# Retention outputs of a block in two visits of TensorE instead of three, and one pair's scores and k^T v' two products earlier

## The chip, the cores and the metric

The kernel runs on one core of a Trainium2 chip. The time is in microseconds on the device, from one execution of the whole program. The profile is of another execution of the same program. In it, TensorE is PE, its weight loads are PEld, VectorE is DVE, ScalarE is ACT, GpSimd is POOL and SyncE, which issues the DMA transfers, is SP. The granted clock of TensorE was 1.000.

## The reference

Two steps follow each other. The first is a retention (linear attention with a decay) over q, k and v of shape 4 x 8 x 768 x 64 (batch, heads, tokens, width of a head):

```python
gamma = 1.0 - 2.0 ** (-5.0 - np.arange(H))
for t in range(S):
    state = gamma * state + einsum('bhd,bhe->bhde', k[:, :, t], v[:, :, t])
    y[:, :, t] = scale * einsum('bhd,bhde->bhe', q[:, :, t], state)
```

Its output becomes x, with 3072 rows (batch and token) and 512 columns (head and width). The second step is two layers with an ELU between them:

```python
h = x @ w_in                                   # 512 -> 2048
g = np.where(h > 0.0, h, np.exp(np.minimum(h, 0.0)) - 1.0)
out = g @ w_out                                # 2048 -> 512
```

All is float32.

## The kernel before, in words

The 3072 tokens are worked on in six blocks of 512 (`TB`). The text calls them the first to the sixth; in the code `tb` is 0 to 5. A block is four chunks of 128 tokens, and two chunks are a pair (`pp` is 0 or 1). The two layers of the first block are plain products. The second block takes one level of Strassen's method in the first layer (`first`) and two in the second (`second_twice`). Blocks three and four, and then five and six, go through together (`big_twice`, `passes`, `second_big`, with `nb` 0 and 1). The large matmuls are 128x128 weights against 128, 256 or 512 columns.

The order of the work is written out by hand. Each engine runs its instructions in the order in which the program emits them. The products are generators: every `yield` is a place where something else can be put between two products.

The retention of a block is put in between like that, while the block or the pair of blocks before it is still in its layers. It works on pieces of 64 tokens, with 64x64 matmuls in two row groups and two column groups of TensorE:

- `scores(tb, pp)`: the products of k and q of a pair (64 small matmuls in the profile for each pair, which it calls `sc`), which VectorE then masks (L342) and writes over k in the chunk's tile.
- `states(tb, pp)`: k^T v' of a pair, where v' is v times a power of the decay (tile `kv`). ScalarE or VectorE add them up to running states (L381, L383).
- `outputs(tb, pp)`: a generator with two stops. To the first it issues `within` (masked scores times v'). To the second it issues `across` for `other` = 0 (q times the state, for two of the four pairings of row group and half). It also lets VectorE copy a few columns of the PSUM tiles `y` into `seen` (L411), for which `across` with `other` = 1 must wait. From there to its end it issues `across` with `other` = 1, and VectorE multiplies `y` by powers of the decay into x (L417).

A pair has two `y` tiles, and `sc`, `kv`, `y` and some results of the layers share the four buffers of the pool `ps_r`. A float32 matmul of the program stands as two matmuls and two weight loads in the profile.

A stretch in which TensorE does only such small matmuls between two products is called a visit here. Before the change the outputs of a block take three visits, by `outputs_step(tb, step)`:

- Blocks two to four (`early_end`): first pair up to its second stop; then the end of the first pair and the second pair up to its second stop; then the end of the second pair.
- Blocks five and six: first pair up to its second stop; second pair up to its second stop; then the ends of both.

`retention_step(tb, n)` calls `scores` for both pairs (n = 0), `states` for both (1), and `outputs_step(tb, n - 2)` for 2 and more. Where these calls stand is said by lists like `VISITS`, whose entries are (number of the product, place in it); places are "first", "middle" and "end". `LOADS` says in the same way where a chunk of the next block is loaded, by a DMA that SP issues (L125), and where GpSimd scales v (L305).

The fourth block's pairs are apart. Before the change `scores(3, 0)` comes when the second block's last product of the second layer has been through its "end" place, and `states(3, 0)`, `scores(3, 1)`, `states(3, 1)` and the outputs come in the first two rounds (`at` = 0 and 1) of the loop over `big_twice`.

Some other names: `bank("a")`, `bank("b")` and `bank("d")` are the PSUM tiles `pa` (two buffers), `pb` and `pd` (one each) of the layers' products. L1376, L1268, L977 and L1330 are matmuls of the layers, L989, L1388 and L1283 are VectorE's additions that read a bank of PSUM, and L944 and L1358 are VectorE's differences that make the inputs of coming products (`ts`, `tq`, `gC`).

Of the kernel before, what the change touches and what calls it, by code (L numbers as in the profile page):

```python
# [28 lines left out]
def kernel(  # L29
# [267 lines left out]
    held = {}  # L297
# [28 lines left out]
    def score_products(sc, tb, pp, x):  # L326
        qk = raw[tb * CPB + 2 * pp + x][0]
        for p in range(HP):
            for sub in range(2):
                for a in range(2):  # L330
                    nc.tensor.matmul(  # L331
                        sc[a][rows(sub), x, p, :], lhsT=qk[rows(a), 1, p, rows(sub)],
                        rhs=qk[rows(a), 0, p, rows(sub)], start=True, stop=True, skip_group_check=True,
                    )

    def scores(tb, pp):

        sc = [ps_r.tile([P, 2, HP, D], FP32, name="sc", tag="r") for _ in range(2)]
        for x in range(2):
            score_products(sc, tb, pp, x)  # L340
        for a in range(2):
            nc.vector.tensor_tensor(  # L342
                out=raw[tb * CPB + 2 * pp + a][0][:, 1].rearrange("p h c -> p (h c)").rearrange("p (n t) -> p n t", t=D),
                in0=sc[a].rearrange("p x h t -> p (x h) t"),
                in1=cmask.unsqueeze(1).to_broadcast([P, 2 * HP, D]), op=ALU.mult,
            )
# [18 lines left out]
    def state_products(kvs, tb, pp, x, subs):  # L365
        kv = raw[tb * CPB + 2 * pp + x][1]
        for p in range(HP):
            for sub in subs:
                for a in range(2):
                    if not fresh(tb, 4 * pp + 2 * x + sub + 1):  # L370
                        nc.tensor.matmul(  # L371
                            kvs[sub][rows(a), x, p, :], lhsT=kv[rows(sub), 1, 2 * p + a, :],
                            rhs=kv[rows(sub), 0, 2 * p + a, :], start=True, stop=True, skip_group_check=True,
                        )

    def state_sum(kvs, tb, pp, x, sub, copy=None):
        n = 4 * pp + 2 * x + sub
        if fresh(tb, n + 1):
            return
        if fresh(tb, n):  # L380
            (copy or nc.scalar.copy)(state(tb, n + 1), kvs[sub][:, x])  # L381
        else:
            nc.vector.tensor_tensor(out=state(tb, n + 1), in0=kvs[sub][:, x], in1=state(tb, n), op=ALU.add)  # L383

    def states(tb, pp):

        kvs = [ps_r.tile([P, 2, HP, D], FP32, name="kv", tag="r") for _ in range(2)]
        for x in range(2):
            state_products(kvs, tb, pp, x, range(2))
        for x in range(2):  # L390
            for sub in range(2):
                state_sum(kvs, tb, pp, x, sub)
# [80 lines left out]
    def outputs_step(tb, step):  # L473

        if step == 0:
            held["y"] = [outputs(tb, pp) for pp in range(2)]
        early_end = tb <= 3
        if step and early_end:
            next(held["y"][step - 1], None)
        elif step == 2:  # L480
            for g in held["y"]:
                next(g, None)
        if step < 2:
            next(held["y"][step])
            next(held["y"][step])

    half = [slice(0, TH), slice(TH, TB)]

# [127 lines left out]
    def small_of_pieces(at):  # L616

        sources = [
            (decoded[2 * NQ + n].rearrange("p r (d c) -> p (r d) c", d=2)[:, 1:4], sums[n])
            for n in (2 * at, 2 * at + 1)  # L620
        ]
        return combine_w_out(at, *sources)
# [915 lines left out]
    y = outputs_of_first()  # L1538
# [40 lines left out]
    y = outputs(0, 1)  # L1579
# [9 lines left out]
    def run(steps):  # L1589
        for _ in steps:  # L1590
            pass

    def next_piece(by_vector=False):
        decode_all()
        prepare(by_vector=by_vector)
# [8 lines left out]
    for n, _ in enumerate(inner):  # L1604
        if n in (0, 2, 4):
            load(CPB + n // 2)
        if n == 4:
            load(CPB + 3)
        if n in (1, 2, 4, 5, 7, 9):
            next_piece(n in (1, 2, 5, 7))  # L1610
        if n == 8:
            scale_v(CPB + 2, True)
        if n in (3, 5, 9):
            scale_v(CPB + (n - 3) // 2)
        if n == 4:
            run(inputs_of_first(0, [hslot() for _ in range(3)]))
        elif n == 10:
            scores(1, 0)
            scores(1, 1)
        elif n == 11:  # L1620
            states(1, 0)
            states(1, 1)
            next_piece()
            parts = sums_of_pieces(0)
            next(parts)
        elif n == 12:
            outputs_step(1, 0)
            run(parts)
            next_piece()
        elif n == 13:  # L1630
            outputs_step(1, 1)
            smalls = small_of_pieces(0)
            some(smalls, 3)
        elif n == 14:
            outputs_step(1, 2)
            some(smalls, 2)
            decode_all()
        elif n == 15:
            run(smalls)
# [40 lines left out]
    def retention_step(tb, step):  # L1680
        if step == 0:
            scores(tb, 0)
            scores(tb, 1)
        elif step == 1:
            states(tb, 0)
            states(tb, 1)
        else:
            outputs_step(tb, step - 2)
# [87 lines left out]
        pass  # L1776
    flush()
    retention_step(2, 2)
    step, VISITS = 0, {(1, "first"): 3, (1, "end"): 4}
    LOADS = {(1, "first"): 0, (2, "end"): 1, (4, "end"): 2, (5, "end"): 3}  # L1780
    for s in sec:
        if s == "first":
            step += 1
        at = (step, s if s in ("first", "middle") else "end")
        if s in ORDER2 and 1 <= step <= 4:
            some(smalls[1], 1 if step < 4 else 3)
        if step == 5:
            send_small(2)
        elif at == (6, "first"):
            sent(1)  # L1790
        if at in VISITS:
            retention_step(2, VISITS[at])
        if at in LOADS:
            load(3 * CPB + LOADS[at])
            scale_v(3 * CPB + LOADS[at])
        if s == ORDER2[-1]:
            break
    scores(3, 0)
    for _ in sec:
        pass  # L1800
    mid.close()
# [5 lines left out]
    for nb in range(NB):  # L1807
        more = nb + 1 < NB
        q6, q4, u3, ends = {}, {}, {}, {}
        groups = 2 * nb + 4, 2 * nb + 5  # L1810
# [79 lines left out]
        for at, (j, sub) in enumerate(ORDER1):  # L1890
            if at == 2:
                held_x = [ldpool.tile([P, 2048], FP32, name="chunk", tag="chunk") for _ in range(2)]
                G["M1"] = [x.rearrange("p (n f t c) -> p n f t c", n=2, f=2, t=2) for x in held_x]
            cur = big_twice(nb, j, sub)
            next(cur)
            if at:
                next(tail, None)
            else:
                run(tail)
                open_lifts()  # L1900
            side(at, 0)
            if at == 1 and nb == 0:
                retention_step(3, 2)
            next(cur)
            side(at, 1)
            if nb == 0:
                if at == 0:
                    states(3, 0)
                elif at == 1:
                    retention_step(3, 3)  # L1910
            run(tail)
            if at == 7:
                seeds(0, 1, first=True)
            next(cur)
            tail = cur
            if nb == 0:
                if at == 0:
                    scores(3, 1)
                    states(3, 1)
                elif at == 1:  # L1920
                    retention_step(3, 4)
                    run(tail)
            side(at, 2)
            if more and at in (5, 6):
                load(groups[0] * CPB + at - 5)
            if nb == 0 and at in stores:
                stores[at]()
                send_small()
# [71 lines left out]
        if more:  # L2000
            for n in range(CPB):
                scale_v(groups[0] * CPB + n)
        step = 0
        VISITS = [
            (0, "end"), (1, "end"), (2, "middle"), (2, "end"), (3, "middle"),
            (5, "first"), (5, "end"), (6, "first"), (6, "middle"), (6, "end"),
        ]
        LOADS = [(3, "middle"), (3, "end"), (4, "first"), (4, "middle")]
        for s in sec:

            if pending:
                pending.pop(0)()
            if s == "first":
                step += 1
            at = (step, s if s in ("first", "middle") else "end")
            if more and at in VISITS:
                n = VISITS.index(at)
                retention_step(groups[n // 5], n % 5)
            if more and at in LOADS:
                bring(groups[1], LOADS.index(at))  # L2020
            if s == BIG2[-1]:
                break
# [56 lines left out]
```

## Time and profile before

| What | Value |
|---|---|
| Time, median of 3 runs | 614.78 us (614.37 to 614.92) |
| Profiled execution, its own time | 612.33 us |
| Its span, first to last instruction | 610.6 us |
| TensorE busy | 602.7 us (99%) |
| Weight loads busy | 492.5 us (81%) |
| VectorE busy | 506.5 us (83%) |
| ScalarE busy | 262.3 us (43%) |
| GpSimd busy | 97.0 us (16%) |
| Small matmuls of retention that are called `sc`, `kv`, `y` | 768, 704 and 1360 (704 at L427, 656 at L442) |

The busy shares are of the span. In the profile's groups, a number such as 128x256 is the partitions and elements of an operand, and 64*64 is the size of the weights. In a timeline a line is a start and a length in microseconds, the engine, the source line, the operation, the tiles written and read, and the count. Square brackets at its end tell for how long the engine was idle just before and what ended that; "issue" is time in which it waited for nothing that the profile shows. Lengths of single matmuls overlap, so the distance of two starts tells more than the length.

### The profile page before, as it was taken

What the parts mean: (1) busy time and instruction counts of PE and PEld (TensorE: products, weight loads), DVE (VectorE), ACT (ScalarE), POOL (GpSimd) and SP (SyncE); (2) the same over time, 40 slices, a digit from 0 to 9 for tenths busy, and PEclk for the clock granted to TensorE, in tenths of its full rate; (3) what the DMA queues carried; (4) which work ended last, traced back from release to release, by engine and by line L of the source; (5) the groups of instructions that cost most, each with busy time, mean ns of one, the idle gap of its engine ahead of it and who ended that gap; (6) DMA issues with size and microseconds to landing.
All of it is one profiled execution on the core that took longest, in us unless ns stands there. A gap on an engine that the chain in (4) does not pass through costs nothing.

```text
span 610.6 us, 13767 instructions
## 1 busy us (share of the span) xinstructions
PE 602.7 (99%) x5510; PEld 492.5 (81%) x5510; DVE 506.5 (83%) x778; ACT 262.3 (43%) x448; POOL 97.0 (16%) x75
## 2 busy tenths in 40 slices
PE   8999999999999999999999999999999999999997
PEld 6765568888889998888766888888888866788886
DVE  5769889989799886889998787898658999778785
ACT  6899744205553112147689310100236778611110
POOL 2011000000220001000697000110000398000000
PEclk9999999999999999999999999999999999999999
DMA  8698569789977999599986455874554676656553
GB/s 318 272 389 308 172 215 270 234 244 259 353 236 242 296 394 325 182 299 258 307 286 222 125 136 156 271 272 115 191 166 154 172 206 191 166 152 188 152 151 116
DMA packets 87856, 139.85 MB, mean 229 GB/s; under 512 B 7024, under 2 KB 48752, under 8 KB 83056
## 3 DMA queue, kind: packets, MB, share of 16 engines
q1 hardware_dynamic: 87792, 138.96, 71.3%
q8 instruction: 44, 0.72, 0.5%
q14 instruction: 20, 0.16, 0.1%
HBM read 105.12 MB, written 33.82 MB: 228 GB/s over the span
## 4 chain that ended last, share of the span: by engine, by line
PE 92%; DMA 3%; DVE 2%; POOL 1%; issue 0%; ACT 0%; ACTq 0%; DVEq 0%
PE pa L1376 16%; PE pa L1268 8%; PE pd L1376 8%; PE pa L977 4%; PE pb L1376 4%; PE pd L1268 4%; PE pa L557 3%; PE x L647 3%; PE pa L784 3%; PE x L1330 3%; PE pa L647 2%; PE pa L1317 2%; PE pb L1268 2%; PE sc L331 2%; PE pd L977 2%; PE kv L371 2%
## 5 line engine op out<-in xcount | busy, mean ns | idle before, releaser
L1384 ACT COPY ms<-pa 128x256 f32<-128x256 f32 x41 | 15.2, 372 | 107.5 <-PE pa L1376 103.0
L1376 PE MATMUL pa<-gC,wq 128*128 128x256 f32 x240 | 56.8, 382 | 0.0
L1376 PEld LDWEIGHTS pa<-gC,wq 128*128 128x128 f32 x240 | 45.1, 190 | 7.2 <-issue 1.0
L305 POOL TENSOR_TENSOR chunk<-chunk,vf 128x512 f32<-128x512 f32 x15 | 19.1, 1278 | 164.9 <-DMA chunk<-in_qkv_dram 120.2
L1343 ACT ACTIVATE r<-r 128x512 f32<-128x512 f32 x64 | 40.4, 631 | 2.0
L1279 ACT COPY m<-pa 128x512 f32<-128x512 f32 x32 | 18.7, 584 | 38.5 <-PE pa L1268 35.1
L1388 DVE TENSOR_TENSOR res<-pd,ms 128x256 f32<-128x256 f32 x26 | 11.0, 422 | 28.2 <-PE pd L1376 17.4
L1376 PE MATMUL pd<-w_all,wq 128*128 128x256 f32 x120 | 28.3, 379 | 0.0
L1344 DVE SCALAR_TENSOR_TENSOR gC<-r,gC 128x512 f32<-128x512 f32 x24 | 27.6, 1158 | 0.0
L925 POOL TENSOR_TENSOR wp<-wp 128x512 fp32r<-128x512 f32 x6 | 8.4, 1404 | 116.3 <-DMA scratch_dram<-wi 102.8
L1376 PEld LDWEIGHTS pd<-w_all,wq 128*128 128x128 f32 x120 | 22.8, 190 | 3.1
L1833 POOL TENSOR_TENSOR chunk<-chunk,w_all 128x512 f32<-128x512 f32 x4 | 5.1, 1298 | 127.1 <-DVE gC L1348 127.1
L183 ACT ACTIVATE w_all<-wraw 128x1024 uint32<-128x1024 uint32 (+1 forms) x19 | 19.1, 1007 | 14.0 <-PE x L647 9.8
L1358 DVE TENSOR_TENSOR gC<-w_all,gC 128x1024 f32<-128x1024 f32 x20 | 24.2, 1260 | 0.0
L1376 PE MATMUL pa<-ts,wq 128*128 128x256 f32 x96 | 22.9, 381 | 0.0
L1376 PE MATMUL pa<-w_all,wq 128*128 128x256 f32 x96 | 22.9, 381 | 0.0
L185 ACT ACTIVATE w_all<-wraw 128x1024 fp8e4<-128x1024 f32 (+1 forms) x19 | 22.6, 1190 | 0.6
L1376 PE MATMUL pd<-ts,wq 128*128 128x256 f32 x96 | 22.7, 379 | 0.0
L557 PE MATMUL pa<-xb,w_all 128*128 128x512 f32 x48 | 21.5, 597 | 0.0
L1410 ACT COPY res<-pa 128x256 f32<-128x256 f32 x13 | 4.8, 372 | 38.1 <-PE pa L1376 38.1
L213 DVE CUSTOM_DVE_ANT_0 w_all<-wraw,w_all 128x2048 uint16<-128x2048 uint16 (+1 forms) x19 | 20.1, 1057 | 0.8
L514 ACT ACTIVATE r<-r 128x512 f32<-128x512 f32 x32 | 20.2, 630 | 1.0
(361 smaller groups left out, 1606.7 us busy)
## 6 DMA issues: line engine op xcount, KB each, us to landing
wq<-scratch_dram SPq DMA_DIRECT2D x231, 256.0 KB, 3.5
chunk<-in_qkv_dram SPq DMA_DIRECT2D x22, 1024.0 KB, 7.3
wraw<-in_w_dram SPq DMA_DIRECT2D x15, 1024.0 KB, 6.1
scratch_dram<-wp SPq DMA_DIRECT2D x8, 512.0 KB, 4.0
out_dram<-res SPq DMA_DIRECT2D x7, 512.0 KB, 3.4
scratch_dram<-gT SPq DMA_DIRECT2D x12, 256.0 KB, 4.3
wq<-scratch_dram SPq DMA_DIRECT2D x24, 128.0 KB, 3.2
scratch_dram<-w_all SPq DMA_DIRECT2D x24, 128.0 KB, 3.0
```

What stands on the lines that cost most here:

```text
L183: nc.scalar.activation(flat, lo, AF.Copy, scale=2.0**-29)
L185: nc.scalar.activation(top, hi.bitcast(FP32), AF.Copy, scale=2.0**-120, saturate=False)
L213: vec.tensor_tensor(out=flat, in0=c, in1=flat, op=ALU.add)
L514: nc.scalar.activation(e, e, AF.Exp, scale=-1.0)
L557: nc.tensor.matmul(hp, lhsT=w[n][:, fi, j // 2, j % 2, :], rhs=xb[:, j, :], start=(j == 0), stop=(j == 3))
L647: nc.tensor.matmul(X[j][:, d, :], lhsT=w[j][:, d * P : d * P + P], rhs=x[j], start=(n == 0 and d == 0), stop=at_end, skip_group_check=True,)
L977: nc.tensor.matmul(ps, lhsT=w[:, f, :], rhs=ts[j][k][:, f, :], start=(begin and f == 0), stop=(f == 3), skip_group_check=True,)
L1268: nc.tensor.matmul(ps[:, f, :], lhsT=w[:, f, :], rhs=big_xs[j][k], start=(begin and f == 0), stop=True, skip_group_check=True,)
L1343: nc.scalar.activation(r, r, AF.Exp, scale=-1.0)
L1344: return lambda: nc.vector.scalar_tensor_tensor(g, r, -1.0, h, ALU.add, ALU.max)
L1358: nc.vector.tensor_tensor(out=quarter(to, r, t), in0=quarter(x, r, t), in1=quarter(y, r, t), op=op)
L1376: nc.tensor.matmul(ps, lhsT=w[:, f, :], rhs=ts[j][k][:, f // 2, f % 2, :], start=(begin and f == 0), stop=(f == 3), skip_group_check=True,)
```

## The change

- `outputs_step`: in step 0 both pairs go to their second stop; in step 1 both end. There is no step 2, so each block has two visits for its outputs, and the first has the work of both pairs up to the wait.
- The second block loses its call for step 2. The third loses its entry for n = 4, so its last visit is the one at (1, "first"). The fourth loses n = 4 as well. Blocks five and six have eight entries in `VISITS` instead of ten, with the last visit of each at (2, "end") and (6, "middle").
- The fourth block's first pair: `scores(3, 0)` moves to (5, "first") and `states(3, 0)` to (6, "first") of the second block's second layer, that is, up by some products. `scores(3, 1)` takes the place that `states(3, 0)` had, and `states(3, 1)` stays where it was, now without `scores(3, 1)` ahead of it in the same visit.

In the built programs the order of instructions on SP and GpSimd is the same. ScalarE's copy of the first state (L381) of the fourth block moves up. VectorE's masks, sums, `seen` copies and multiplications by powers move with the visits: four `seen` copies and four multiplications now stand together in each block.

```diff
@@ outputs_step
         if step == 0:
             held["y"] = [outputs(tb, pp) for pp in range(2)]
-        early_end = tb <= 3
-        if step and early_end:
-            next(held["y"][step - 1], None)
-        elif step == 2:
+            for g in held["y"]:
+                next(g)
+                next(g)
+        else:
             for g in held["y"]:
                 next(g, None)
-        if step < 2:
-            next(held["y"][step])
-            next(held["y"][step])
@@ second block
         elif n == 14:
-            outputs_step(1, 2)
             some(smalls, 2)
@@ third and fourth block
-    step, VISITS = 0, {(1, "first"): 3, (1, "end"): 4}
+    step, VISITS = 0, {(1, "first"): 3}
...
         if at in VISITS:
             retention_step(2, VISITS[at])
+        if at == (5, "first"):
+            scores(3, 0)
+        elif at == (6, "first"):
+            states(3, 0)
...
-    scores(3, 0)
...
                 if at == 0:
-                    states(3, 0)
+                    scores(3, 1)
                 elif at == 1:
                     retention_step(3, 3)
...
                 if at == 0:
-                    scores(3, 1)
                     states(3, 1)
                 elif at == 1:
-                    retention_step(3, 4)
                     run(tail)
@@ fifth and sixth block
         VISITS = [
-            (0, "end"), (1, "end"), (2, "middle"), (2, "end"), (3, "middle"),
-            (5, "first"), (5, "end"), (6, "first"), (6, "middle"), (6, "end"),
+            (0, "end"), (1, "end"), (2, "middle"), (2, "end"),
+            (5, "first"), (5, "end"), (6, "first"), (6, "middle"),
         ]
...
-                retention_step(groups[n // 5], n % 5)
+                retention_step(groups[n // 4], n % 4)
```

## The prediction

> **What bounds the kernel now.** I read the page's busy shares and chain first, then TensorE's and its weight loads' timelines around the 64x64 work, then VectorE's there.
>
> ```profile
> PE 602.7 (99%) x5510; PEld 492.5 (81%) x5510; DVE 506.5 (83%) x778; ACT 262.3 (43%) x448; POOL 97.0 (16%) x75
> ...
> q8 instruction: 44, 0.72, 0.5%
> ...
> PE 92%; DMA 3%; DVE 2%; POOL 1%; issue 0%; ACT 0%; ACTq 0%; DVEq 0%
> ```
>
> TensorE works without a break and carries 92% of the chain that ended last, so a change is worth what it adds to or takes from TensorE's own sequence. Queue 8 carries instructions, 16.4 KB a packet.
>
> TensorE's timeline in the fifth block (start, length, then the group):
>
> ```profile
> 340.21 1.89 PE L1376 MATMUL pa<-gC,wq 128*128 128x256 f32 x8
> 342.03 2.10 PE L331 MATMUL sc<-chunk 64*64 64x64 f32 x128
> 344.06 1.99 PE L1376 MATMUL pa<-w_all,wq 128*128 128x256 f32 x8
> ...
> 382.69 1.89 PE L1376 MATMUL pd<-ts,wq 128*128 128x256 f32 x8
> ```
>
> Groups of eight start every 1.73 us. From 340.21 to the group at 345.89 there are 5.68 us: two groups (3.46) and a visit of 128 small matmuls, 2.22. From 382.69 to 387.42 there are 4.73: two groups and a visit of 56, 1.27. The 56 take 0.876 us from first to last load, as 64 do elsewhere (0.889): a skipped matmul leaves its slot empty. So 64 slots cost 0.95, 14.8 ns each, and **a visit costs 0.33 us beyond its slots**.
>
> Weight loads of the fourth block:
>
> ```profile
> 242.67 1.00 PEld L331 LDWEIGHTS sc<-chunk 64*64 64x64 f32 x58 [0.33 <-issue]
> 244.22 0.20 PEld L331 LDWEIGHTS sc<-chunk 64*64 64x64 f32 x6 [0.54 <-issue]
> ...
> 247.47 0.83 PEld L427 LDWEIGHTS y<-chunk 64*64 64x64 f32 x49 [0.33 <-DVE chunk L383]
> 248.97 0.32 PEld L427 LDWEIGHTS y<-chunk 64*64 64x64 f32 x15 [0.66 <-issue]
> ```
>
> The 0.33 is the way into a visit. The 0.54 and 0.66 are not: they stand inside a run of equal matmuls and wait for nothing shown. Counting TensorE's records (loads, matmuls, semaphore waits) in order of start, the two pauses come at records 5570 and 5826, 256 apart; so do two small ones of the start, at 962 and 1218, and 1218 to 5570 is 17 times 256. Queue 8's packets, one for each batch of 256 records, fit: each starts near the crossing of such a boundary, and **all four pauses end 1.33 to 1.48 us after the packet's end**. From the trace's records (us; "usable" is the end plus 1.4):
>
> ```
> boundary, crossed | next packet: start, takes | usable after crossing
> 1986   70.52      |  71.56  1.40              | 3.84
> 4034  191.76      | 193.86  0.96              | 4.46
> 5570  244.22      | 246.65  0.96              | 4.79 (paused for it)
> 5826  248.97      | 250.10  1.11              | 3.64
> 7874  371.22      | 371.76  1.06              | 3.00
> 9154  423.60      | 424.01  1.24              | 3.05
> ```
>
> For the 16 boundaries that are crossed in 64x64 work it is 3.05 to 5.11 us, mean 4.1. A batch is 128 small matmuls, 1.87 us at 14.6 ns. So TensorE eats a batch of small matmuls faster than the next comes. Before the change no visit is long enough to hold two boundaries, except the third block's scores at 173.91, which met one after 5 records and the next 5 records behind their end; their packet had started at 172.00, during slow matmuls.
>
> **The change part by part.** The order of PE's instructions in both builds gives the visits and the record numbers.
>
> *Visits.* Blocks two, three, five and six go from three output visits to two, with the same slots (192 and 64): 4 x 0.33 = -1.3 us. Block four loses one of outputs but its scores and k^T v' of the second pair part: six visits before and after, nothing.
>
> *Old pauses.* Block four's first pair moves up among the slower 128-wide groups. The batch 5570 to 5826 then holds two visits and 3 groups, by the rows of before 5.0 us against 3.64 to 4.79: no pause. The two gaps (0.68 and 0.80 from load to load) go: -1.45 us.
>
> *New pauses.* The first output visit now has 184 to 192 small matmuls, 2.8 us.
> - Block two: boundary 1986 comes 36 loads into it, 2242 at 164. Between them 1.87 us, and the packet is usable after 3.84: a wait of **1.97**.
> - Block three: 4034 at load 72; the next boundary is 14 records behind the visit: 1.75 + 0.2 (way out) + 7 x 0.11 = 2.73 against 4.46: **1.73**.
> - Block four: 5826 at load 48, 6082 at 176: 1.87 against 3.64: **1.77**.
> - Block five: 7874 at load 98, the next at load 34 of the second visit, behind a group: 1.3 + 0.3 + 1.73 + 0.5 = 3.8 against 3.0: none.
> - Block six: 9154 at load 38, 9410 at 166: 1.87 against 3.05: **1.18**.
>
> Together +6.65. At the mean of 4.1 it would be 8.0, at the shortest 3.9, at the longest 12; I take the rows of the same boundaries, since their crossing is the same.
>
> [...]
>
> *VectorE behind the second visit.* `across(.., 1)` waits for the `seen` copies. In block five they are queued behind this:
>
> ```profile
> 367.24 4.62 DVE L1358 TENSOR_TENSOR gC<-w_all,gC 128x1024 f32<-128x1024 f32 x4
> 371.78 1.22 DVE L944 TENSOR_TENSOR ts<-gC 128x1024 f32<-128x1024 f32 x1
> 373.03 1.23 DVE L944 TENSOR_TENSOR ts<-gC,ts 128x1024 f32<-128x1024 f32 x1
> 374.17 0.23 DVE L411 COPY seen<-y 128x8 f32<-128x8 f32 x2
> ```
>
> Four copies end at about 374.55. TensorE comes back after visit (368.91 + 2.8 + 0.2) and one group (1.73 + 0.3): 373.9. It waits 0.5 to 0.6, where before it came at 384.5: **+0.55**. In the other blocks the copies are done first (block six 428.9 against 429.8 without the pause). In block four the four multiplications (L417, 0.62 each, 2.5 us) now stand ahead of the addition that frees `pa` (L1283, 0.68): done 3.2 us after the visit, needed after 2.8: **+0.45**. In block three the same kind of row (`res<-pd`, needed by the next product 7) is ready 0.2 us early: nothing, at worst 0.4.
>
> *Inputs of the earlier scores.* The fourth chunk of block four is issued by SP at 233.67 and lands at 241.9. Its first use, 0.47 into the second pair's scores, moves from 243.1 to about 242.2: behind the group that ends at 240.4, plus the 1.2 of the first pair's k^T v', which is now ahead. If SP's queue, whose transfers partly wait for TensorE, slips by that visit (1.2 us), TensorE waits 0.9; if not, nothing. I take +0.3. The order of SP and POOL is the same in both builds, and ScalarE's only moves one copy.
>
> **Sum:** -1.3 - 1.45 + 6.65 + 0.55 + 0.45 + 0.3 = +5.2. A little may vanish where TensorE waits for ScalarE or GpSimd anyway (gaps of about 1 us in all at 167 to 170 and 296 to 300): +5.0. The profiled execution is 612.33 (span 610.6) and would be 617.3; the median of the runs is 614.78, 2.45 higher, and would be **619.8**.
>
> **Rivals.**
> 1. *Faster: batches do not run out.* If more than one is on hand when a visit begins, the new pauses stay away and the old ones go: -1.3 - 1.45 + 1.3 = -1.45, 613.3; without the waits on VectorE 612.0. For it: the scores at 173.91 ate a batch in 2.55 us with no pause. Against it: that one's packet had ended at 172.98, and the pauses at 5570 and 5826. It decides from a usable time below 1.9 us; none of the 16 is under 3.05. [...] 0.11.
> 2. *Same: losses and gains cancel.* If packets start sooner in the longer runs, so that all are usable after 3.05, and those of two visits even before they are missed, two pauses of 1.2 are left: 2.4 + 0.55 + 0.45 - 2.75 = +0.65, 615.4. Block six's 3.05 is for it, the mean of 4.1 against. 0.06.
> 3. *Slower by more*: pauses at the mean of 4.1 and the chunk late: +7.2, 622.0; part of the forecast.
> 4. *The change doesn't do what it says*: the order of instructions shows two output visits per block, so no chance.
>
> **How the numbers follow.** The measurement tells about 0.2% (1.2 us) from no change. The forecast, with the pauses at all sizes, has 0.83; of it nothing is faster. So faster 0.11, same 0.06, slower 0.83. The four pauses vary by about 0.6 each, 1.2 together, the other terms by about 0.7: 619.8 -2.5/+3.2, the upper end with all four at the mean of 4.1. Downward the range takes in rival 2: 615.2 to 623.0. Alone, the forecast's range is 617.3 to 623.0.
>
> **What would show it.** Right: in the first output visit of blocks two, four and six, weight loads of `y` with 1 to 2.5 us "<-issue" in the middle, and one of the 128-wide groups right behind that of block three; no such pause in block four's scores; a `seen` wait of about 0.5 us in block five; visits one fewer in four blocks. Wrong: visits of 2.8 us without a pause, which leaves rival 1, or pauses that end otherwise than about 1.4 us after a packet of queue 8.

## The result, and the profile after

| | before | changed |
|---|---|---|
| Median of the runs | 614.58 us (611.47 to 615.03, 6 runs) | 620.4 us (616.87 to 625.26, 6 runs) |
| Profiled execution, its own time | 612.33 us | 616.87 us |
| Its span | 610.6 us | 615.1 us |

The changed kernel is slower, by a ratio of 1.0111 (95% interval 1.0065 to 1.0157). The two profiled executions differ by 4.5 us. Ratios, here and below, leave out three executions that were over 1.5% longer than the fastest of their kernel (630.83 and 626.16 us of e2, 626.77 us of e12); the medians count them.

The lines of the page of the changed kernel that answer to those of before:

```profile
PE 602.2 (98%) x5510; PEld 492.4 (80%) x5510; DVE 507.3 (82%) x778; ACT 262.3 (43%) x448; POOL 97.1 (16%) x75
...
q8 instruction: 44, 0.72, 0.5%
...
PE 92%; DVE 5%; issue 1%; POOL 1%; ACT 0%; DVEq 0%
```

TensorE has the same 5510 matmuls and nearly the same busy time (602.2 us, before 602.7); the span grew around them. "issue" went from 0% to 1% of the chain: time in which TensorE waited for nothing that the profile shows. The timeline of weight loads tells where it is, in the first output visits of blocks two, three, four and six:

```profile
72.18 0.19 PEld L442 LDWEIGHTS y<-chunk 64*64 64x64 f32 x3
74.08 0.48 PEld L442 LDWEIGHTS y<-chunk 64*64 64x64 f32 x21 [1.71 <-issue]
...
194.53 0.86 PEld L974 LDWEIGHTS pa<-ts,wq 128*128 128x128 f32 x7
197.06 0.19 PEld L974 LDWEIGHTS pa<-ts,wq 128*128 128x128 f32 x1 [1.68 <-issue]
...
252.54 0.48 PEld L442 LDWEIGHTS y<-chunk 64*64 64x64 f32 x19
254.55 0.25 PEld L442 LDWEIGHTS y<-chunk 64*64 64x64 f32 x9 [1.53 <-issue]
...
429.23 0.20 PEld L442 LDWEIGHTS y<-chunk 64*64 64x64 f32 x5
430.25 0.54 PEld L442 LDWEIGHTS y<-chunk 64*64 64x64 f32 x27 [0.82 <-issue]
```

Three pauses stand among equal small matmuls, after 163, 175 and 165 of a visit's weight loads (forecast: 164, 176, 166). The one of block three stands behind its visit, after seven loads of the next group. The merged visit of block five (184 loads in 2.756 us) has none, and the two old pauses of block four are gone. TensorE's waits, with their sum, number and longest:

```profile
PE y L442 <- issue: 3.6, 3, 1.6
PE pa L974 <- issue: 1.6, 1, 1.6
...
PE y L442 <- DVE seen L411: 0.9, 2, 0.6
...
PE pa L974 <- ACT ms L982: 0.4, 1, 0.4
```

The third line is block five. VectorE's timeline there, and then TensorE's:

```profile
370.81 4.62 DVE L1355 TENSOR_TENSOR gC<-w_all,gC 128x1024 f32<-128x1024 f32 x4
375.35 1.22 DVE L941 TENSOR_TENSOR ts<-gC 128x1024 f32<-128x1024 f32 x1
376.60 1.23 DVE L941 TENSOR_TENSOR ts<-gC,ts 128x1024 f32<-128x1024 f32 x1
377.74 0.53 DVE L411 COPY seen<-y 128x8 f32<-128x8 f32 x4
```

```profile
375.44 1.99 PE L1373 MATMUL pa<-gC,wq 128*128 128x256 f32 x8
378.03 0.27 PE L442 MATMUL y<-chunk 64*64 64x64 f32 x2 [0.59 <-DVE seen L411]
```

The products that the copies read were done at 375.4, but six passes of 128x1024 stand ahead of the four copies on VectorE, so TensorE waits 0.59 us past its next group; from load to load the way into the visit is 1.19 us where it was 0.52.

### The profile page after: what moved, and what is told of

Same layout as the page of the kernel before. It is cut to its first block, busy times and chain, and to the rows that moved or that the text cites. A ratio compares the mean times of both kernels' runs of the same rounds, so it can differ in the third digit from the quotient of the medians.

```text
span 615.1 us, 13777 instructions
## 1 busy us (share of the span) xinstructions
PE 602.2 (98%) x5510; PEld 492.4 (80%) x5510; DVE 507.3 (82%) x778; ACT 262.3 (43%) x448; POOL 97.1 (16%) x75
## 4 chain that ended last, share of the span: by engine, by line
PE 92%; DVE 5%; issue 1%; POOL 1%; ACT 0%; DVEq 0%
PE pa L1373 15%; PE pa L1265 9%; PE pd L1373 7%; PE pa L781 5%; PE pb L1373 4%; PE pd L1265 4%; PE pa L554 3%; PE x L644 3%; PE pa L974 3%; PE x L1327 3%; PE pd L781 2%; PE pa L644 2%; PE pa L1314 2%; PE pb L1265 2%; PE kv L371 2%; PE sc L331 2%
```

## The experiments

Theory A is that of the prediction: TensorE's records come in batches of 256 (11,251 records and 44 packets before), a new batch is usable some 1.4 us after the end of its packet on queue 8 (1.33 to 1.48 before), and a visit that reaches a boundary before that pauses there. It adds that this happens where a visit holds two boundaries. The rivals: the visit's length itself is the cause, or VectorE, or the half of the change that moves block four's first pair.

**The two halves apart.** e3_move_only keeps three visits and moves the first pair of block four:

```diff
 outputs_step: as before the change (three visits in every block)
+        if at == (5, "first"):
+            scores(3, 0)
+        elif at == (6, "first"):
+            states(3, 0)
...
```

> Three output visits per block as before, with the fourth block's first pair moved up as in the change. Theory A: the two pauses of block four go (-1.45), one visit more (+0.33), 0.35 of a wait of TensorE for ScalarE's copy that the earlier k^T v' brings: -0.8 us, span 609.8, no pause over 0.3 us inside a visit of blocks two to six. Rival (the early pair costs, by its chunk or by VectorE): 611 or more.

e2_merge_only merges the visits and leaves block four's first pair where it was:

```diff
-        if at == (5, "first"):
-            scores(3, 0)
-        elif at == (6, "first"):
-            states(3, 0)
...
 outputs_step: as in the changed kernel
```

> Two output visits per block, with the fourth block's first pair where it was before. Theory A: visits -1.65, new pauses of 1.8, 1.6, 1.8 and 1.0 in blocks two, three, four and six, one at block four's old places (0.7 in the scores and 0.8 at the head of the outputs) as before the change, the wait for seen in block five 0.7: +5.2 us, span 615.8. Rival B: about 614 to 616 as well, but without pauses inside the output visits. If the pair's place were what costs: at or below 611.

The move alone took 612.56 us, ratio 0.9982 [0.9966, 0.9997]; merging alone 621.38 us, 1.0103 [1.0072, 1.0134]. So the loss is the merging's, and the move is a small gain. Weight loads of block four with the move alone:

```profile
242.44 1.02 PEld L331 LDWEIGHTS sc<-chunk 64*64 64x64 f32 x64 [0.33 <-issue]
...
247.61 0.83 PEld L427 LDWEIGHTS y<-chunk 64*64 64x64 f32 x49 [0.33 <-issue]
248.88 0.32 PEld L427 LDWEIGHTS y<-chunk 64*64 64x64 f32 x15 [0.44 <-issue]
```

The pause in the scores is gone, one of 0.44 us is left in the outputs here, and there is none in any other visit behind block one's. It stands at a boundary, 1.28 us after a packet's end, and 5.0 us of work lie between it and the boundary before. In e6 and e9 below, with the same boundary, it is missing too.

**The boundaries moved.** e1_shifted is the changed kernel, e4_before_shifted the kernel before, with 72 records fewer at the very start:

```diff
-    for n in range(25):
+    unread(1, TH)
+    for n in range(6):
         nc.tensor.matmul(
```

> The changed kernel with 19 of the 25 unread small matmuls of the start replaced by one unread matmul of 256 columns: 72 fewer records of TensorE ahead of all else, so that every boundary of 256 records falls 72 records later in the work, and nothing else is moved. Theory A (a merged visit waits for its next batch of instructions): the boundaries then stand 145 records into the first output visit of block two, 215 into block three's, 169 into block four's, 13 into block five's and 149 into block six's, and none of the visits holds a full batch any more, so the four pauses (1.83 + 1.59 + 1.65 + 0.95 = 6.0 us) go, but for 0 to 0.4 us in blocks five and six: span 609 to 610 us against 615.1, and faster than the kernel before (610.6). Rival B (the merged visits cost because of VectorE's later work or the longer stretch itself): nothing moves but the start, span 614 to 615.5.

> The kernel before with the same replacement at the start as in the shifted run of the changed kernel. It says what the replacement does by itself. Theory A: block four's boundary falls 188 records into its scores and k^T v' visit instead of 116, a pause of about 0.8, and 170 into the first output visit, none: 0.6 us less than before, and with the start 609.5 to 611. Rival B: like the kernel before within 0.5 us, with both pauses of block four at the same matmuls as before.

e1 took 618.33 us (ratio 1.0087 [1.0055, 1.0119]), e4 617.88 us (1.0077 [1.0054, 1.0099]). The times were not what I expected, the pauses' places were by the count: in e1 none of the four first output visits pauses (2.772, 2.756 and 2.773 us in blocks two, four and six; 0.14 us in block three), with as many small matmuls as before. But visits elsewhere now paused, though each held only one boundary. In e1 this was block one's outputs, and in e4 block four's k^T v', neither of them touched by the change:

```profile
24.88 0.43 PEld L427 LDWEIGHTS y<-chunk 64*64 64x64 f32 x18
27.22 0.38 PEld L427 LDWEIGHTS y<-chunk 64*64 64x64 f32 x19 [1.91 <-issue]
```

```profile
247.00 0.56 PEld L371 LDWEIGHTS kv<-chunk 64*64 64x64 f32 x29
249.44 0.66 PEld L371 LDWEIGHTS kv<-chunk 64*64 64x64 f32 x35 [1.88 <-issue]
```

In the records these two, two others of 1.53 and 1.56 us in block two, and one of 1.97 us in block one of e4 end with the matmul and the load numbered 193 and 194 modulo 256, as the pauses of before do, and 1.29 to 1.56 us after a packet's end. (Another, of 0.93 us in block six's scores of e1, waits for a chunk's DMA.) Between each of these boundaries and the one before lie 3.0 to 5.7 us of work. The opposite case is in e1 too: block five's first output visit holds two boundaries, at 373.95 and 375.82, only 1.87 us apart, and does not pause:

```profile
375.24 1.03 PEld L427 LDWEIGHTS y<-chunk 64*64 64x64 f32 x64
376.19 0.55 PEld L442 LDWEIGHTS y<-chunk 64*64 64x64 f32 x24
376.80 0.73 PEld L1373 LDWEIGHTS pa<-gC,wq 128*128 128x128 f32 x4
```

Its packet had started at 373.16, ahead of the first of the two, and taken 0.93 us; by the 1.4 us it was usable at 375.5. My expectation had looked only at the visits of the change, and had overlooked this second boundary. What follows: the pause goes with the record's number and the packet's time, not with the kind or the length of a visit, nor with two boundaries in one visit as such.

**The same, in one place.** e12_fill_six is the changed kernel with 96 records more in block six, nothing before it moved:

```diff
             score_products(sc, tb, pp, x)
+        for x in range(2 if (tb, pp) == (5, 1) else 0):
+            score_products(sc, tb, pp, x, 3)
```

The new argument, 3, makes three of the four products over `p`.

> The changed kernel, with 24 of block six's score products (second pair) done twice: 96 more records just before its k^T v' and outputs, and nothing moved before. Theory A: the boundary that stood at load 38 of the first output visit now comes some 20 records before it, and the next at about load 118 instead of 166, with over 4 us of work between them: the pause of block six (0.96 in the profiled execution of the changed kernel, 1.63 in that of e5) goes, those of blocks two, three and four stay as they are. Net of the 0.70 us of the doubled products: 0.3 to 0.9 less than the changed kernel, near 619.8. Rival B (a visit of 192 small matmuls pauses after some 165 of them): the pause of block six stays at load 166, +0.7: 621.1.

618.29 us, ratio 1.0067 [1.0044, 1.009]. Block six's first output visit, 192 loads, has no pause (2.771 us), and those of blocks two (1.57), three (behind the visit) and four (1.56) stay:

```profile
430.63 1.05 PEld L429 LDWEIGHTS y<-chunk 64*64 64x64 f32 x64
431.56 0.58 PEld L444 LDWEIGHTS y<-chunk 64*64 64x64 f32 x32
432.21 1.59 PEld L1375 LDWEIGHTS pa<-gC,wq 128*128 128x128 f32 x8
```

That a visit pauses by its length is out. This execution also showed the late chunk of block four, which the profiled execution of the changed kernel had not:

```profile
247.26 0.56 PEld L331 LDWEIGHTS sc<-chunk 64*64 64x64 f32 x32 [1.24 <-DMA chunk<-in_qkv_dram]
```

**The wait for `seen`.** e5_five_ends_later is the changed kernel with one entry later:

```diff
-            (0, "end"), (1, "end"), (2, "middle"), (2, "end"),
+            (0, "end"), (1, "end"), (2, "middle"), (3, "middle"),
```

> The changed kernel, with the second output visit of block five one product later, at (3, "middle"). Theory A (batches of 256 records, and the wait for the `seen` copies in block five because VectorE is behind): the way into that visit goes back from 1.19 us to 0.52, nothing else moves, and the four pauses of 1.0 to 1.9 us stay: 0.67 us less than the changed kernel, near 619.7. Rival B (the 0.67 us are no wait for VectorE but belong to the visit): the way in stays at 1.19 us, time as the changed kernel, 620.4.

The way into that visit was 0.52 us again, as theory A has it. The time was 621.65 us (ratio 1.0126 [1.0095, 1.0158]): a saving of 0.67 us cannot be told within the spread of these pauses. Block six's was 1.58 us here, against 0.90 in the changed kernel.

**Merging where it fits.** e6_merge_five_only has the moved pair of e3, and two visits in block five alone:

```diff
+        if tb == 4:
+            for g in held["y"]:
+                next(g, None)
+                if step == 0:
+                    next(g)
+            return
 block five's entries:
-            (2, "middle"), (2, "end"), (3, "middle"),
+            (2, "middle"), None, (3, "middle"),
```

> e3_move_only, with the output visits of block five merged (both pairs to their second stop at (2, "middle"), both ends at (3, "middle")), all other blocks with three visits. Theory A: only the merged visits that hold two boundaries less than some 3 us apart pause, and block five's does not, so merging here costs nothing and saves one visit: 0.33 us less than e3_move_only in the trace, about 612.2. Rival B (any visit of 184 small matmuls pauses, by 1 to 2 us): 613.9.

612.63 us, ratio 0.9971 [0.9946, 0.9997]: no pause and no wait in block five (184 loads in 2.756 us, then 0.52 into the second visit). Its profiled execution has two other pauses at boundaries: 0.86 us in block one's outputs and 1.07 us among the large matmuls of block three, at 205.03. There 5.0 us of work lie between two boundaries, and the packet, started at 201.19, took 2.41 us instead of about 1.

**Two visits, cut elsewhere.** e7_late_by_scalar and e8_late_by_vector have the moved pair of e3, and in blocks two to six (`LATE`) they put the second pair and both ends into the second visit, 96 and 160 slots:

```diff
+        g = held["y"]
+        if step < 2:
+            next(g[step])
+            next(g[step])
+        if tb in LATE and step == 1:
+            next(g[0], None)
+            next(g[1], None)
 in outputs, e7 alone:
+                    if pp and tb in LATE:
+                        nc.scalar.copy(seen..., y[sub][:, :, :, 0])
```

> e3_move_only, with another split into two visits in blocks two to six: first pair to its second stop (96 slots); later, second pair to its second stop, end of the first pair, end of the second (160 slots). The `seen` copies of the second pair are made by ScalarE. Theory A: five visits fewer, -1.65 us; no visit holds two boundaries with less than 4 us of work between them, so no pauses; TensorE now waits inside the second visit for the copies, about 0.7 us after the last product they read less 0.47 of the first pair's end, 0.25 each, +1.25: about 612.2. Rival B (long visits pause whatever the boundaries): 5 pauses of 1 to 2 us, 617 to 620. Rival C (ScalarE is behind when the copies come up, by 1 us each): 616.

> As e7_late_by_scalar, with the `seen` copies of the second pair on VectorE as in the kernels before. Theory A: no pauses, five visits fewer (-1.65 us); VectorE, 82% busy, has other work queued when the copies come up, as in block five, where TensorE waited 0.67: about 0.5 to 1.5 us each inside the second visit, +2.5 to +7.5: 613.5 to 618.5, slower than e7_late_by_scalar. If it is the same as e7_late_by_scalar, the queue of VectorE does not matter at these places.

e7: 613.86 us, 0.9989 [0.9971, 1.0008]. e8: 617.91 us, 1.0059 [1.0033, 1.0086]. No output visit of blocks two to six paused at a boundary. (Elsewhere e7 had a gap of 0.54 us, where 0.11 is usual, at a boundary among block three's large matmuls, and e8 one of 0.31 us in block one's outputs.) In e7 the waits for ScalarE were 0.07 to 0.14 us a block (expected: 0.25), but block five waited 0.71 for the first pair's copies, which are VectorE's. In e8 the waits were 0.08 to 0.50, except block five, where one of 0.71 is followed by a longer one:

```profile
373.59 0.33 PEld L442 LDWEIGHTS y<-chunk 64*64 64x64 f32 x16
376.11 0.54 PEld L442 LDWEIGHTS y<-chunk 64*64 64x64 f32 x24 [2.19 <-DVE seen L411]
```

VectorE's queue at this place costs more (0.71 and 2.33 us from load to load) than the five visits save (1.65). e9_best takes what paid: e6's block five, e7's cut in the other four.

```diff
+    LATE = (1, 2, 3, 5)
```

> e6_merge_five_only, with the split of e7_late_by_scalar in blocks two, three, four and six (block five keeps the merged visit of e6). Theory A: four visits fewer than e6_merge_five_only, -1.32 us; waits inside the second visits as e7_late_by_scalar showed them (0.07, 0.13, 0.14, 0.13), +0.47; no pauses: 0.85 us less than e6_merge_five_only, about 611.8. Rival: the waits for ScalarE take the 0.33 of each visit back, no difference.

611.31 us, ratio 0.9961 [0.9937, 0.9986], faster than the kernel before and the changed one; its waits inside the visits were 0.07, 0.13, 0.14 and 0.13 us as in e7, and no output visit of blocks two to six paused. Whether it is faster than e6, the intervals do not tell.

**The clock.** In the timed runs of the changed kernel the mean clock was 1.000 only in the fastest (616.87); in the others it was .997 to .999. The profile of e1 (clock .997) has one stretch of 3.413 us at clock 0.5, beginning 1.8 us after its pause of 2.04 us; e8 has one, 0.9 us after the wait of 2.3 us. To see whether an idle TensorE brings that about, e10_wait_short and e11_wait_long are e6 with a wait put into block six that has nothing to do with instructions:

```diff
 block six cut as in e7; ahead of its `seen` copies on ScalarE:
+                        for _ in range(12):        # e11: 32
+                            nc.scalar.copy(seen..., y[sub][:, :, :, 0])
```

> e6_merge_five_only, with block six as in e7_late_by_scalar and 12 more `seen` copies on ScalarE ahead of the two that TensorE waits for (the output is the same): a wait of TensorE of about 1.5 us that has nothing to do with instructions. Theory C (the clock is halved for the 3.413 us behind a stretch of 3.413 us in which TensorE was idle for 1.88 us or more, whatever it waited for): no drop of the clock; -0.33 + 1.5: 613.8.

> As e10_wait_short with 32 more copies: a wait of about 3.8 us. Theory C: a stretch of 3.413 us at clock 0.5 behind it in every execution (mean clock .997), which costs 1.7 us more: 612.6 - 0.33 + 3.8 + 1.7 = 617.8. Rival D (drops of the clock come from something else that late instructions bring with them, or from chance): clock 1.000 in most executions, 616.1.

A copy took 0.20 us of ScalarE where I had reckoned 0.115, so the waits were 2.49 and 6.46 us. e10: 615.26 us (ratio 1.0028 [1.0005, 1.005]); e11: 621.9 us (1.0115 [1.0075, 1.0154]). e11 by stretches, first e10's for comparison; the columns are the stretch, its length, the busy time and instructions of PE, PEld, DVE, ACT and POOL, then the granted clock, the share of DMA and GB/s:

```profile
428.40:431.80 3.40, 1.64 (x113) 1.50 (x104) 2.72 (x7) 1.85 (x12) 0.00 (x0) 1.00 1.02 351
431.80:435.20 3.40, 2.95 (x43) 2.62 (x44) 1.29 (x2) 0.66 (x4) 0.00 (x0) 1.00 0.23 77
```

```profile
432.50:435.90 3.40, 0.18 (x13) 0.04 (x4) 1.29 (x3) 2.87 (x18) 0.00 (x0) 1.00 0.73 243
435.90:442.70 6.80, 3.84 (x39) 3.18 (x40) 1.29 (x2) 2.47 (x16) 0.00 (x0) 0.50 0.01 3
442.70:450.00 7.30, 7.30 (x35) 6.26 (x33) 2.68 (x4) 1.85 (x4) 0.00 (x0) 1.00 0.32 92
```

e10's wait is split by a border of these stretches; TensorE was idle for 1.78 us of the one and 0.44 of the next, and the clock stayed. In e11 two stretches that follow each other were idle for 3.23 and 2.95 us, and the clock was 0.5 in the stretch behind each, 6.83 us together. All four executions of e11 had a mean clock of .992 to .995, seven of ten of e10 .999 or 1.000. Rival D (chance, or something that only late instructions bring) is out for a wait of this length.

## Why the prediction was right

It gave 619.8 us (617.3 for a profiled execution); 620.4 and 616.87 were measured. Step by step, on the profiled execution (pauses from weight load to weight load, that of block three as TensorE's idle time):

| Step | forecast | measured |
|---|---|---|
| Visits, four fewer | -1.3 | -1.3 (not measured one by one; from the starts of its groups, block five saved 0.35) |
| Old pauses of block four | -1.45 | gone, -1.45 |
| New pause, block two | 1.97 | 1.84 |
| block three | 1.73 | 1.59 |
| block four | 1.77 | 1.67 |
| block five | 0 | 0 |
| block six | 1.18 | 0.96 |
| `seen` in block five | 0.55 | 0.67 |
| The addition behind four multiplications, block four | 0.45 | 0.15 |
| The chunk of block four | 0.3 | 0 (0.1 to 1.4 us in e6, e7, e12) |
| Not foreseen: TensorE for `ms` (L982) at 239.57 | 0 | 0.35 |
| Sum | +5.2 | +4.5 |

- *New pauses.* They ended as forecast, some 1.4 us after a packet's end: 1.46, 1.43, 1.51 and 1.12 us (1.33 to 1.48 before). Rival 1 is out by these four pauses: batches do run out. Its condition, a packet started early, does occur (block five of e1). That a visit pauses where it holds two boundaries fits the changed kernel; it is no rule, since e1 and e4 paused in visits with one, and e1 did not in a visit with two.
- *Their size.* I took the rows of the same boundaries, since their crossing is the same. That held on the average and not one by one. The same four pauses, from record to record in us, with e2's profiled execution the longest of its runs (630.83):

```
              two    three  four   six
changed       1.78   1.87   1.61   0.90
e5            1.51   2.04   1.39   1.58
e2            2.38   1.44   1.12   3.05
```

The packet starts when it starts: at block six 0.4, 0.7 and 2.5 us after the crossing of the boundary before. "About 0.6 each" was too narrow; one of six executions (625.26) lies above the range. The prediction had made the spread look smaller than it was: its 16 boundaries in 64x64 work leave out three others of the kernel before, at 173.93 (which it names as an exception), at 183.00, whose packet started 3.4 us after the crossing (usable after 5.9), and at 356.45, whose packet started 0.29 us ahead of it (usable after 2.0). With them the usable time goes from 0.5 to 5.9 us, not from 3.05 to 5.11. What sets a packet's start stays open.
- *Block four.* The wait for the multiplications was smaller than put, and the cover of the chunk is as thin as the prediction said: 0 or some 1 us, by execution.
- *From the profiled execution to the median.* I added 2.45 us because before's median lay that far above its profile. It was 3.5, and partly for a reason that the step did not know: in the other executions the clock fell. A stretch of 3.413 us at half the clock costs some 1.7 us (an estimate: half of it), and is .0028 of the mean clock, which is the .997 of four of them. So 619.8 met 620.4 partly by a sum of terms of which two were off in opposite ways (the sum, taken at +5.0, by 0.4 too large, this step by 1.1 too small).
- *Rivals.* Rival 2 (two pauses only) is out by four pauses. Rival 3's condition, the chunk late, came in e12, with the pauses near their forecast.

## What to carry to other kernels

A saving in TensorE's small matmuls is to be counted in instructions as well as in time: put the boundaries of 256 records over the visits, and where two of them fall into a few microseconds of work, expect a pause. Over the fourteen traces, past the first 18 us, a boundary with less than 2.2 us of work between it and the one before had a pause of 0.3 us or more in 11 of 12 cases, with 2.2 to 4 us in 19 of 49, with 4 to 6 us in 5 of 92. So in these traces distance helps, but no distance up to 6 us rules a pause out, since a packet can start late (3.4 us after the crossing at 183.00 of the kernel before) or take long (2.41 us in e6). Cut the visits so that the boundaries fall into different ones (e9) rather than make them few; and let the signal that TensorE waits for come from an engine with an empty queue (outside block five, 0.07 to 0.14 us of waiting for ScalarE in e7, 0.08 to 0.50 for VectorE in e8). Any early change in the count moves all later boundaries, so a gain or loss of 0.5% may come from places that the diff does not touch (e4: 72 records fewer at the start, 0.8% slower).

## What the runs showed of the hardware that was not expected

In the traces of this case the granted clock changes at the borders of stretches of 3.413 us that run through from start to end: all the lengths between changes are whole multiples (23.893 is 7 of them, 372.053 is 109; the one stretch at 1.0 is 604.159 before, 177 of them, and 607.572 in the changed kernel, 178). A stretch in which TensorE was idle (no matmul in the profile) for 1.88, 1.94, 2.05 (twice), 2.17, 2.95 or 3.23 us was followed by one at 0.5; idle for 1.57, 1.59, 1.74, 1.76 or 1.78 us, by one at 1.0. So by these traces the bound lies between 1.78 and 1.88 us of 3.413, a little over half, whether the wait was for instructions (e1, e2) or for another engine (e8, e11). The timed runs do not confirm it as sharply. If the border can fall anywhere, some six of ten executions of e10 (idle for 2.22 us) should have had 1.83 us or more in one stretch, an estimate from ((3.413 - 2.22) + 2 x (2.22 - 1.83)) / 3.413 = 0.58; three of ten had a clock of .996 or .997. At half the clock e8's matmuls of L1383 start 0.43 us apart, and 0.21 us behind that stretch. So a pause of 2 us would cost 2 us in one execution and, by the estimate of 1.7 us above, 3.7 us in another, by where the border of the stretches falls; no pair of runs shows this on one and the same pause.
